# Column groups inside the K block, fewer zero matmuls, a modulation in two pieces and other wo banks, in an adaLN block of linear attention and GeGLU

## The chip, the cores and the metric

The kernel runs on one NeuronCore of a Trainium2 chip. The metric is the device time of one execution in microseconds. The engines are named as in the profile: PE is TensorE (PEld its weight loads), DVE is VectorE, ACT is ScalarE, POOL is GpSimd. The granted clock is the share of its full clock that TensorE was given, as the trace records it (1.0 is full, 0.5 is half; 128x512 matmuls start 0.216 us apart at 1.0 and 0.43 us apart at 0.5). A DMA lands when its data has arrived; to evict a PSUM bank is to read its result out of it, so that the bank can be written again.

## The reference, cut to what matters

```python
mod = (silu(c) @ w_mod).reshape(1, 6, 1, -1)        # sa, ca, ga, sb, cb, gb
h = layernorm(x) * (1 + ca) + sa                    # x: 2048 x 1024
x = x + ga * linear_attention(h, wqkv, wo)          # 32 heads, phi(t) = elu-like + 1e-6
h = layernorm(x) * (1 + cb) + sb
x = x + gb * (gelu(h @ w_gate) * (h @ w_up) @ w_down)   # F = 3584
```

The change touches the first half only: how sa and ca come about as columns, the K and V products of the first four chunks (128 rows each), the modulation of chunks 14 and 15, and the PSUM banks of the product with wo.

## The kernel before: the parts that matter

Work is recorded in program order, one in-order stream for each engine, and waits follow from the tiles that operations share. Where an operation stands in its engine's stream therefore matters as much as what it depends on: in the changed kernel one add of 0.16 us, standing early in DVE's stream, kept DVE idle for 2.25 us, and the work recorded behind it waited too.

```python
def mod_cols(q, bank):          # shift/scale of quarter q: 256 columns each, as 4 PSUM columns
    for t in range(2):
        for b in range(2):
            for dc in range(8):
                matmul(PS(bank, col, col + 1), WMQ[q][:, dc, t, b*128:(b+1)*128], SILUT[:, dc:dc+1], ...)
    DVE: MODT[:, q*4:q*4+4] = PS(bank, ...) + ADD4                              # L575

def warm(n, bank):              # n zero matmuls 128x512: they only keep PE active    L667
def mod1(c0, n, dc0, dc1):      # DVE: h1T = h1T * scale + shift, for each dc          L542
def k_part(q, cs):              # K matmuls of quarter q (dc = 2q, 2q+1) of chunks cs   L611
def xhat_dve(c), ln1_bn(c, h)   # DVE: normalise chunk c (L498); bn_stats of one half (L673)

# the head (cut)
t1(1, 6)                        # 8 PE transposes of chunk 1
warm(7, 7)
ln1_bn(2, 1); ln1_fin(2); ln1_bn(3, 0)
xhat_dve(2); t1(2, 7)
mod_cols(0, 4); mod1(0, 2, 0, 2)
...
warm(1); k_part(1, [0, 1, 2, 3])
warm(2)
mod_cols(2, 4); mod1(0, 4, 4, 6)
warm(1); k_part(2, [0, 1, 2, 3])
...
# the loop over chunks 4 to 15 (cut)
for _ in range({13: 1, 14: 1, 15: 0}.get(c_, 2)):
    q_block(...)                # takes the next of 4 PSUM banks; DVE evicts it (L601, L603)
# two K blocks, two V blocks, each in the next bank: with one q block, the second V reuses q's bank
if c_ % 2 == 1 and c_ + 2 < NCH:
    mod1(c_ + 1, 2)             # chunks c_+1 and c_+2 in one piece, 256 columns
if c_ == 13:
    ...                         # POOL builds the tile SEL: an iota and 4 tensor_scalar (L803)
if c_ >= 12:
    ...                         # DVE: two folds of wo with ga (L810)
# w2_pair(g): two matmuls into banks 2 and 3 (L840), ACT copies them to W2 (L842)
for c_ in range(12):
    wo_chunk(c_, 2 * ((c_ + 1) % 2))    # banks 2/3 first, then 0/1, ...             L928
```

Of the kernel before, what the change touches and what calls it, by code (L numbers as in the profile page):

```python
# [216 lines left out]
def bass_adaLN_cond__linear_attn_block__geglu_ffn__prompt_kernel(  # L217
# [14 lines left out]
    with ExitStack() as es:  # L232
# [264 lines left out]
        def xhat_dve(c_, dst, rng):  # L497
            sch.op(V, lambda e: e.tensor_scalar(dst[:, :], XALL[:, c_, :], MVA[:, c_, 0:1], RSA[:, c_:c_ + 1],  # L498
                                                op0=ALU.subtract, op1=ALU.mult),
                   rd=r_x(c_) + r_smc("mv", c_, 8) + r_smc("rs", c_, 4), wr=rng, note=f"xhat {c_}")  # L500
# [5 lines left out]
        def xh_buf(c_):  # L506
            i = c_ % 3
            return XH[i], r_2k(XHO[i], f"xh{i}")
# [10 lines left out]
        def t1(c_, tb):  # L519
            b_, rng = xh_buf(c_)  # L520
            sg, ci = divmod(c_, CPG)
            for dc in range(NDC):
                sch.op(T, lambda e, dc=dc: e.transpose(PS16(tb, dc * P, (dc + 1) * P), b_[:, dc * P:(dc + 1) * P], IDENT[:, :]),
                       rd=rng + r_sm("ident"), pwr=pr(tb), note=f"T1 {c_}.{dc}")
            sch.op(A, lambda e: e.activation(H1[sg][:, :, ci * P:(ci + 1) * P], PS16(tb).rearrange("p (a b) -> p a b", a=NDC), ACTF.Copy),
                   prd=pr(tb), wr=r_h1(sg, 0, NDC, ci * P, (ci + 1) * P), note=f"h1raw {c_}")
# [26 lines left out]
        def mod1(c0, n, dc0=0, dc1=NDC):  # L553
            sg, ci = divmod(c0, CPG)
            mods(H1, r_h1, sg, sc1, ci * P, (ci + n) * P, dc0, dc1, "h1")
# [109 lines left out]
        def warm(n, bank=None):  # L665
            for _ in range(n):
                sch.op(T, lambda e: e.matmul(PS(0 if bank is None else bank), WARM[:, 0:P], WARM[:, :], start=bank is not None,  # L667
                                             stop=bank is not None, skip_group_check=True),
                       rd=R_WARM, pwr=pr(bank) if bank is not None else (), note="warm")
# [5 lines left out]
        def ln1_fin(c_):  # L675
            sch.op(V, lambda e: e.bn_aggr(MVA[:, c_, :], STA[:, c_, :]), rd=r_smc("st", c_, 48), wr=r_smc("mv", c_, 8), note=f"aggr A{c_}")
            sch.op(V, lambda e: e.tensor_scalar(VEA[:, c_:c_ + 1], MVA[:, c_, 1:2], 1e-5, None, op0=ALU.add),
                   rd=r_smc("mv", c_, 8), wr=r_smc("ve", c_, 4), note=f"ve A{c_}")
            sch.op(G, lambda e: e.tensor_tensor(RSA[:, c_:c_ + 1], VEA[:, c_:c_ + 1], NEGHALF[:, :], ALU.pow),
                   rd=r_smc("ve", c_, 4) + r_sm("neghalf"), wr=r_smc("rs", c_, 4), deps=[last_g[0]], note=f"rstd A{c_}")  # L680
# [19 lines left out]
        ln1_bn(2, 0)  # L700
        xhat_dve(1, *xh_buf(1))
        t1(1, 6)
        warm(7, 7)
        ln1_bn(2, 1)
        ln1_fin(2)
        ln1_bn(3, 0)
        xhat_dve(2, *xh_buf(2))
        t1(2, 7)
        mod_cols(0, 4)
        mod1(0, 2, 0, 2)  # L710
        ln1_bn(3, 1)
        ln1_fin(3)
        k_part(0, [0, 1])
        xhat_dve(3, *xh_buf(3))
        mod1(2, 1, 0, 2)
        t1(3, 7)
        k_part(0, [2])
        mod1(3, 1, 0, 2)
        warm(3)
        k_part(0, [3])  # L720
        mod_cols(1, 4)
        mod1(0, 4, 2, 4)
        warm(1)
        k_part(1, [0, 1, 2, 3])
        warm(2)
        mod_cols(2, 4)
        mod1(0, 4, 4, 6)
        warm(1)
        k_part(2, [0, 1, 2, 3])
        warm(2)  # L730
        mod_cols(3, 4)
        mod1(0, 4, 6, 8)
        warm(1)
        k_part(3, [0, 1, 2, 3])
        for (c_, jg), b in kb0.items():
            k_evac(c_, jg, b)
# [26 lines left out]
        for c_ in range(4, NCH):  # L763
            if c_ % 4 == 0:
                q_todo += [(c_ // 4 - 1, qc) for qc in range(NG)]
            for _ in range({13: 1, 14: 1, 15: 0}.get(c_, 2)):
                q_block(*q_todo.pop(0))
            for jg in range(2):
                b = nb()
                kv_mm(c_, "k", jg, b, list(range(NDC)))  # L770
                k_evac(c_, jg, b)
            for jg in range(2):
                b = nb()
                kv_mm(c_, "v", jg, b, list(range(NDC)))
                v_evac(c_, jg, b)
            if c_ % 2 == 1 and c_ + 2 < NCH:
                mod1(c_ + 1, 2)
            kvacc(c_ - 1)
            if c_ + 3 < NCH:
                ln1(c_ + 3)  # L780
                t1d(c_ + 3)
            if c_ == 6:
                o_r = mod_rows(0, 4)
                for k, t in enumerate((6, 7, 8, 9)):
                    wm_dma(t, k)
                sch.dma(Q, lambda e: e.dma_start(GAB[:, :].rearrange("p (a b) -> p a b", a=2),
                                                 scr_row[0, 0:2, :].rearrange("(o a) b -> o a b", o=1).to_broadcast([P, 2, 512])),
                        wr=R_GAB, deps=[o_r], note="gab")
                sch.dma(Q, lambda e: e.dma_start(GBB[:, :].rearrange("p (a b) -> p a b", a=2),
                                                 scr_row[0, 2:4, :].rearrange("(o a) b -> o a b", o=1).to_broadcast([P, 2, 512])),  # L790
                        wr=R_GBB, deps=[o_r], note="gbb")
            if c_ == 9:
                o_r = mod_rows(1, 4)
                sch.dma(Q, lambda e: e.dma_start(SBT[:, :], scr_row[1, 0:2, :].rearrange("a (b p) -> p (a b)", p=P)),
                        wr=r_sm("sbT"), deps=[o_r], note="sbT")
                sch.dma(Q, lambda e: e.dma_start(CBT[:, :], scr_row[1, 2:4, :].rearrange("a (b p) -> p (a b)", p=P)),
                        wr=r_sm("cbT"), deps=[o_r], note="cbT")
                sch.dma(Q, lambda e: e.dma_start(WO[:], wo_v), wr=[(OFF_WS, OFF_WS + 16384, "wo")], note="wo")
            if c_ == 13:
                gop(lambda e: e.iota(IOTA_B[:].rearrange("p (a b d) -> p a b d", a=NG, b=HPG), [[4, NG], [1, HPG], [0, 32]],  # L800
                                     channel_multiplier=-1), wr=R_IOTA2)
                for k in range(4):
                    gop(lambda e, k=k: e.tensor_scalar(SEL[32 * k:32 * (k + 1)].rearrange("p a b -> p (a b)"), IOTA_B[32 * k:32 * (k + 1), :],  # L803
                                                       float(-32 * k), None, op0=ALU.is_equal), rd=R_IOTA2, wr=R_SEL)
            if c_ == 11:
                sch.op(V, lambda e: e.tensor_scalar(CB1T[:, :], CBT[:, :], 1.0, None, op0=ALU.add), rd=r_sm("cbT"), wr=r_sm("cb1T"))
            if c_ >= 12:
                for kc in range((c_ - 12) * 2, (c_ - 12) * 2 + 2):
                    rg = [(OFF_WS + kc * 2048, OFF_WS + (kc + 1) * 2048, "wo")]
                    sch.op(V, lambda e, kc=kc: e.tensor_tensor(WO[:, kc, :], WO[:, kc, :], GAB[:, :], ALU.mult),  # L810
                           rd=rg + R_GAB, wr=rg, note=f"wofold {kc}")
# [156 lines left out]
        for q in (4, 5, 6):  # L968
            wd_dma(q)
        for c_ in range(12):  # L970
            wo_chunk(c_, 2 * ((c_ + 1) % 2))
            if c_ == 0:
                den(1, 4)
            if c_ in (2, 3, 5, 6):
                bcast(1, (2, 3, 5, 6).index(c_))
            if c_ < 4:
                ln2_a(c_, False)
            if c_ == 9:
                mod2(0, 2)
                mod2(2, 2)  # L980
# [60 lines left out]
        for q in range(4):  # L1041
            hook(0, 5 + q, lambda q=q: wd_dma(q))
        for sg in range(NSG):
            gu_i[0] = 1 if sg == 0 else 0
            for fp in range(NFP):
                if fp + 2 < NFP and not (sg == 0 and fp == 0):
                    stream_pair(sg, fp + 2)
                ffn_fc(sg, 2 * fp)
                ffn_fc(sg, 2 * fp + 1)
                for fn in hooks.get((sg, fp), ()):  # L1050
                    fn()
            if sg + 1 < NSG:
                stream_pair(sg + 1, 0)
                stream_pair(sg + 1, 1)
            for ci in range(CPG):
                if sg + 1 < NSG:
                    n0 = (sg + 1) * CPG
                    if ci < 2:
                        ln2_a(n0 + 2 * ci, True)
                        ln2_a(n0 + 2 * ci + 1, True)  # L1060
                    else:
                        mod2(n0 + 2 * (ci - 2), 2)
                ffn_down(sg, ci)
# [74 lines left out]
```

## Time and profile before

| | before |
|---|---|
| time, median of 4 executions | 855.52 us (855.51 to 855.53) |
| PE busy | 837.3 of 853.6 us |
| first K matmul to first V matmul | 13.71 to 35.14 us |
| chunk 14's 16 K matmuls, to the first V matmul | 163.26 to 168.08 us |
| last w2 matmul to first wo matmul | 209.60 to 211.22 us |

From the profile's page: the busy time of the engines, and the chain of waits by engine.

```profile
PE 837.3 (98%) x4276; PEld 389.4 (46%) x4359; DVE 496.3 (58%) x881; ACT 294.8 (35%) x483; POOL 38.0 (4%) x73
...
PE 93%; DVE 4%; issue 1%; ACT 1%; POOL 0%; DMA 0%; SPq 0%; ACTq 0%; POOLq 0%
```

PE bounds the kernel. Where it runs freely, 128x512 matmuls start 0.216 us apart (their own 0.38 us overlap), so only places where this pitch is broken can be gained. Here is the head, in the timeline of PE (start, length, engine, line, operation, out<-in, shapes, count, and in brackets the idle time before it and its releaser):

```profile
9.59 1.67 PE L667 MATMUL ps_all<-warm 128*128 128x512 bf16 x7
11.37 0.62 PE L523 MATMUL ps_all<-ident,xh 128*128 128x128 bf16 x8
11.83 0.94 PE L569 MATMUL ps_all<-siluT,wmq 128*128 128x1 bf16 x32
13.71 1.67 PE L611 MATMUL ps_all<-wk,h1T 128*128 128x512 bf16 x7 [0.94 <-DVE h1T L542]
...
23.62 0.94 PE L569 MATMUL ps_all<-siluT,wmq 128*128 128x1 bf16 x32
24.43 0.38 PE L667 MATMUL ps_all<-warm 128*128 128x512 bf16 x1
25.50 2.97 PE L611 MATMUL ps_all<-wk,h1T 128*128 128x512 bf16 x13 [0.69 <-DVE h1T L542]
...
35.14 1.03 PE L611 MATMUL ps_all<-wv,h1T 128*128 128x512 bf16 x4
```

In every quarter PE computes the columns and then waits for DVE to put them onto h1T. In quarters 1 to 3 a zero matmul stands in between, although matmuls of the quarter before could have filled that time. The second place is around chunk 13 and 14, in the timeline of all engines:

```profile
154.09 11.68 POOL L803 TENSOR_SCALAR sel<-iota_b 32x1024 bf16<-32x1024 int32 x4
154.21 3.18 DVE L810 TENSOR_TENSOR wo<-wo,gab 128x1024 bf16<-128x1024 bf16 x2
...
157.31 1.25 DVE L601 TENSOR_SCALAR eb<-eb 128x512 f32<-128x512 f32 x1
...
158.60 0.69 DVE L603 SCALAR_TENSOR_TENSOR pq<-ps_all,eb 128x512 bf16<-128x512 f32 x1
...
162.10 3.82 DVE L542 TENSOR_SCALAR h1T<-h1T,modt 128x256 bf16<-128x256 bf16 x8
...
164.17 1.16 PE L611 MATMUL ps_all<-wk,h1T 128*128 128x512 bf16 x4 [0.31 <-DVE h1T L542]
...
165.91 2.33 PE L611 MATMUL ps_all<-wk,h1T 128*128 128x512 bf16 x10 [0.59 <-DVE h1T L542]
...
168.08 3.62 PE L611 MATMUL ps_all<-wv,h1T 128*128 128x512 bf16 x16
```

DVE reaches the modulation of chunk 14 only at 162.10, and the 16 K matmuls take 4.82 us instead of 16 x 0.216 = 3.45: 1.37 us are lost. L601 took 1.25 us while POOL built SEL (a mask for a later product); at 168.11, without POOL beside it, it took 0.41. The third place is the start of wo, in the timeline of PE:

```profile
209.39 0.59 PE L840 MATMUL ps_all<-wo,kvt 128*128 128x512 bf16 x2
211.22 2.12 PE L928 MATMUL ps_all<-w,pq 128*128 128x512 bf16 x8 [1.23 <-ACT w L842]
```

The first wo chunk uses banks 2 and 3, which ACT is still emptying: 1.62 us from start to start instead of 0.22.

### The profile page before, as it was taken

What the parts mean: (1) busy time and instruction counts of PE and PEld (TensorE: products, weight loads), DVE (VectorE), ACT (ScalarE), POOL (GpSimd) and SP (SyncE); (2) the same over time, 40 slices, a digit from 0 to 9 for tenths busy, and PEclk for the clock granted to TensorE, in tenths of its full rate; (3) what the DMA queues carried; (4) which work ended last, traced back from release to release, by engine and by line L of the source; (5) the groups of instructions that cost most, each with busy time, mean ns of one, the idle gap of its engine ahead of it and who ended that gap; (6) DMA issues with size and microseconds to landing.
All of it is one profiled execution on the core that took longest, in us unless ns stands there. A gap on an engine that the chain in (4) does not pass through costs nothing.

```text
span 853.6 us, 11465 instructions
## 1 busy us (share of the span) xinstructions
PE 837.3 (98%) x4276; PEld 389.4 (46%) x4359; DVE 496.3 (58%) x881; ACT 294.8 (35%) x483; POOL 38.0 (4%) x73
## 2 busy tenths in 40 slices
PE   7999999999999999999999999999999999999998
PEld 3454444443444444444444444444444444444445
DVE  5577667978674455564365666445666535655512
ACT  2233333335513344430245443035454204454300
POOL 2010000600200000000000001000000100000000
PEclk9999999999999999999999999999999999999999
DMA  9981924003523368341355534145553305555000
GB/s 281 362 257 26 272 32 117 13 1 96 178 74 99 99 199 254 109 117 44 112 153 149 149 99 100 36 120 158 157 159 106 72 25 154 149 149 147 6 20 25
DMA packets 179911, 104.06 MB, mean 122 GB/s; under 512 B 32520, under 2 KB 171912, under 8 KB 179856
## 3 DMA queue, kind: packets, MB, share of 16 engines
q1 hardware_dynamic: 179856, 103.33, 43.5%
q8 instruction: 35, 0.57, 0.3%
q14 instruction: 20, 0.16, 0.1%
HBM read 92.28 MB, written 4.21 MB: 113 GB/s over the span
## 4 chain that ended last, share of the span: by engine, by line
PE 93%; DVE 4%; issue 1%; ACT 1%; POOL 0%; DMA 0%; SPq 0%; ACTq 0%; POOLq 0%
PE ps_all L997 23%; PE ps_all L1022 23%; PE ps_all L994 21%; PE ps_all L611 11%; PE ps_all L928 6%; PE ps_all L652 6%; DVE h1T L542 1%; PE ps_all L633 1%; DVE eb L601 0%; PE ps_all L868 0%; PE ps_all L583 0%; DVE xh L498 0%; DVE st L673 0%; DMA xall<-in_A_x_dram 0%; DVE pq L881 0%
## 5 line engine op out<-in xcount | busy, mean ns | idle before, releaser
L997 PE MATMUL ps_all<-h2T,wu 128*128 128x512 bf16 x896 | 339.6, 379 | 1.7
L994 PE MATMUL ps_all<-h2T,wg 128*128 128x512 bf16 x863 | 327.1, 379 | 0.0
L1022 PE MATMUL ps_all<-wd,yT 128*128 128x512 bf16 (+1 forms) x906 | 193.2, 372 | 0.9
L1005 ACT ACTIVATE q<-ps_all 128x512 f32<-128x512 f32 x112 | 66.9, 597 | 235.2 <-PE ps_all L994 231.3
L1022 PEld LDWEIGHTS ps_all<-wd,yT 128*128 128x128 bf16 x924 | 90.4, 98 | 103.3
L994 PEld LDWEIGHTS ps_all<-h2T,wg 128*128 128x128 bf16 x896 | 87.7, 98 | 105.8 <-issue 0.2
L997 PEld LDWEIGHTS ps_all<-h2T,wu 128*128 128x128 bf16 x896 | 87.7, 98 | 105.7
L1007 DVE SCALAR_TENSOR_TENSOR ww<-q,ps_all 128x512 f32<-128x512 f32 x112 | 77.0, 688 | 92.5 <-ACT guh L1006 92.5
L1010 DVE SCALAR_TENSOR_TENSOR ww<-th,guh 128x512 f32<-128x512 f32 x112 | 77.5, 692 | 77.9 <-ACT th L1009 77.9
L1009 ACT ACTIVATE th<-ww 128x512 f32<-128x512 f32 x112 | 70.5, 629 | 84.4 <-DVE ww L1007 84.4
L1012 DVE TENSOR_TENSOR yT<-ww,ps_all 128x512 bf16<-128x512 f32 x112 | 76.8, 686 | 3.8
L1027 DVE TENSOR_TENSOR ps_all<-ps_all,gbb 128x512 f32<-128x512 f32 (+1 forms) x33 | 22.5, 682 | 94.8 <-PE ps_all L1022 94.8
L600 ACT ACTIVATE eb<-ps_all 128x512 f32<-128x512 f32 x64 | 37.5, 601 | 85.0 <-PE ps_all L611 43.6
L1006 ACT ACTIVATE guh<-ps_all 128x512 f32<-128x512 f32 x112 | 66.2, 591 | 0.0
L611 PE MATMUL ps_all<-wk,h1T 128*128 128x512 bf16 x250 | 58.1, 379 | 3.9 <-DVE h1T L542 3.7
L928 PE MATMUL ps_all<-w,pq 128*128 128x512 bf16 x246 | 56.2, 379 | 1.9 <-ACT w L842 1.2
L611 PE MATMUL ps_all<-wv,h1T 128*128 128x512 bf16 x254 | 57.6, 379 | 0.1
L652 PE MATMUL ps_all<-h1T,wq 128*128 128x512 bf16 x243 | 56.6, 379 | 1.0 <-issue 0.3
L601 DVE TENSOR_SCALAR eb<-eb 128x512 f32<-128x512 f32 x64 | 28.8, 449 | 29.7 <-ACT eb L600 29.2
L611 PEld LDWEIGHTS ps_all<-wk,h1T 128*128 128x128 bf16 x256 | 24.6, 98 | 33.6 <-DVE h1T L542 5.7
L928 PEld LDWEIGHTS ps_all<-w,pq 128*128 128x128 bf16 x256 | 24.6, 98 | 31.6 <-ACT w L842 1.7
L611 PEld LDWEIGHTS ps_all<-wv,h1T 128*128 128x128 bf16 x256 | 24.9, 98 | 29.9 <-DVE pq L603 0.3
(87 smaller groups left out, 423.3 us busy)
## 6 DMA issues: line engine op xcount, KB each, us to landing
wg<-in_B_w_gate_dram SPq DMA_DIRECT2D x56, 512.0 KB, 3.9
wu<-in_B_w_up_dram SPq DMA_DIRECT2D x56, 512.0 KB, 5.2
wmst<-in_w_mod_dram SPq DMA_DIRECT2D x8, 1024.0 KB, 11.7
wd<-in_B_w_down_dram SPq DMA_DIRECT2D x7, 1024.0 KB, 7.8
wmq<-in_w_mod_dram SPq DMA_DIRECT2D x8, 512.0 KB, 6.7
out_dram<-xall SPq DMA_DIRECT2D x31, 128.0 KB, 1.7
xall<-in_A_x_dram SPq DMA_DIRECT2D x3, 1024.0 KB, 12.3
wk<-in_A_wqkv_dram SPq DMA_DIRECT2D x4, 512.0 KB, 8.2
```

What stands on the lines that cost most here:

```text
L611: o = sch.op(T, lambda e, dc=dc: e.matmul(PS(bank), H1[sg][:, dc, ci * P:(ci + 1) * P], W_[:, dc, jg * 512:(jg + 1) * 512], start=(dc == 0 ...
L652: o = sch.op(T, lambda e, dc=dc: e.matmul(PS(b), WQ[:, dc, qc * P:(qc + 1) * P], H1[sg][:, dc, :], start=(dc == 0), stop=(dc == NDC - 1)), ...
L928: last[half] = sch.op(T, lambda e, g=g, half=half: e.matmul(PS(b0 + half), PQ[sg][:, g, ci * P:(ci + 1) * P], W2[:, g, half * 512:(half + ...
L994: og = sch.op(T, lambda e, dc=dc: e.matmul(PS(bg), WG[slot][:, dc, e_ * P:(e_ + 1) * P], H2[sg][:, dc, :], start=(dc == 0), stop=(dc == ND ...
L997: ou = sch.op(T, lambda e, dc=dc: e.matmul(PS(bu), WU[slot][:, dc, e_ * P:(e_ + 1) * P], H2[sg][:, dc, :], start=(dc == 0), stop=(dc == ND ...
L1005: sch.op(A, lambda e: e.activation(Q1[j][:, :], PS(bg), ACTF.Square, scale=math.sqrt(GELU_A)), prd=pr(bg), wr=rq, note=f"q1 {fc}")
L1006: ogh = sch.op(A, lambda e: e.activation(GUH[j][:, :], PS(bg), ACTF.Copy, scale=0.5), prd=pr(bg), wr=rg, note=f"gh {fc}")
L1007: sch.op(V, lambda e: e.scalar_tensor_tensor(WW[j][:, :], Q1[j][:, :], 1.0, PS(bg), op0=ALU.add, op1=ALU.mult), rd=rq, prd=pr(bg), wr=rw, ...
L1009: sch.op(A, lambda e: e.activation(TH[j][:, :], WW[j][:, :], ACTF.Tanh, scale=GELU_C), rd=rw, wr=rt, note=f"th {fc}")
L1010: sch.op(V, lambda e: e.scalar_tensor_tensor(WW[j][:, :], TH[j][:, :], 1.0, GUH[j][:, :], op0=ALU.add, op1=ALU.mult), rd=rt + rg, wr=rw, n ...
L1012: sch.op(V, lambda e: e.tensor_tensor(YT[:, fc, :], WW[j][:, :], PS(bu), ALU.mult), rd=rw, prd=pr(bu), wr=r_yt(fc), note=f"yT {fc}")
L1022: o = sch.op(T, lambda e, b=b, fc=fc, c0=c0, c1=c1, n=n: e.matmul(PS(b, 0, n), YT[:, fc, ci * P:(ci + 1) * P], WDT[fc // 4][:, fc % 4, c0:c1],
```

## The change

Its intent: compute the columns of the next quarter in the middle of the K matmuls of the present one, so that the trip over DVE is covered by useful matmuls, and drop the zero matmuls that filled it; bring chunk 14's modulation forward, as a piece of its own; begin wo in free banks. The diff, cut to its core, with the cut marked:

```diff
         t1(1, 6)
-        warm(7, 7)
+        warm(1, 7)
+        mod_cols(0, 4)
         ln1_bn(2, 1)
         ln1_fin(2)
         ln1_bn(3, 0)
         xhat_dve(2, *xh_buf(2))
+        mod1(0, 2, 0, 2)
         t1(2, 7)
-        mod_cols(0, 4)
-        mod1(0, 2, 0, 2)
 ...                                  # [cut: chunks 2 and 3 of quarter 0, same idea, warm(3) dropped]
         warm(1)
-        k_part(1, [0, 1, 2, 3])
-        warm(2)
+        k_part(0, [3])
+        k_part(1, [0, 1, 2])
         mod_cols(2, 4)
         mod1(0, 4, 4, 6)
+        k_part(1, [3])
         warm(1)
-        k_part(2, [0, 1, 2, 3])
-        warm(2)
+        k_part(2, [0, 1])
         mod_cols(3, 4)
         mod1(0, 4, 6, 8)
-        warm(1)
+        k_part(2, [2, 3])
         k_part(3, [0, 1, 2, 3])
@@ loop over chunks
+            if c_ == 13:
+                mod1(14, 1)
             for _ in range({13: 1, 14: 1, 15: 0}.get(c_, 2)):
                 q_block(*q_todo.pop(0))
@@
-                mod1(c_ + 1, 2)
+                mod1(*((15, 1) if c_ == 13 else (c_ + 1, 2)))
@@ wo
-            wo_chunk(c_, 2 * ((c_ + 1) % 2))
+            wo_chunk(c_, 6 if c_ == 0 else 2 * (c_ % 2))
@@ first gate/up pair of banks
-            gu_i[0] = 1 if sg == 0 else 0
+            gu_i[0] = 0
```

## The prediction

> **What bounds it.** TensorE. The page gives PE 837.3 of 853.6 us busy (98%), clock 1.0, and the chain of waits is 93% PE. In the timeline dense 128x512 matmuls start 0.216 us apart, so only places where the pitch is broken can give time. I see three that the change touches.
> 1. Head (first K block): matmuls start at 13.71 us, V starts at 35.14 us: 21.4 us. Inside are 64 K matmuls (13.8 us), 8 transposes (0.45), three column groups (0.9 each), so 4.4 us are zero matmuls (10 x 0.216) and waits for the scale/shift (list of waits: 3.7 us in 6 waits, partly elsewhere).
> 2. Chunk 14: its K matmuls wait for the DVE modulation (L542); 16 take 4.82 us (163.26 to 168.08) instead of 3.45: 1.37 us lost.
> 3. First wo chunk: starts at 211.22, 1.62 us after the last w2 matmul, waiting for ACT to empty banks 2/3 (L842): 1.40 us lost.
>
> **Costed.**
> Head. The first column group moves before T1(2) and its add (L575) stands before bn_stats of chunk 2 on DVE. Weight columns wmq0 land only at 10.7 us (DMA issues: 6.4 and 7.6 us to landing), so DVE waits from 9.1 to about 11.3, xhat(2) moves from 10.77 to about 13.3, and K begins about 0.6 us LATER (14.3). After that each group runs as soon as its PE slot comes, ahead of the quarter's last matmuls, and 8 of 10 zero matmuls go. Stepping through with trace durations (group to column 1.2 us, column to first matmul 0.67 us): quarter 1 at 19.6, quarter 2 at 24.1, quarter 3 at 28.0 (was 30.38), V at 32.8. Landings permit it (wmq2 20.9, wmq3 25.1, x4-7 36.2 us; wv estimated 29.9 and 33.1). Gain 2.3 us, all critical.
> wo. Chunk 0 in banks 6/7 starts at once; W2[7] is ready (211.2) before its last two matmuls. Gain 1.4 us. Re-dealing the others is symmetrical.
> Chunk 14. Splitting makes 8 extra DVE operations (128 columns, 0.22 us pitch each, hardly cheaper than 256 columns at 0.26). mod(14) now stands before chunk 13's q eviction. There DVE is already behind (xhat 15, two wo folds until 157.3), and GpSimd builds SEL 154.1 to 165.8: L601 takes up to 1.25 us instead of 0.42. [...] The second V block of chunk 13 uses q's bank and already starts just as that eviction ends (159.34). Estimate: mod(14) takes 2.8 us there, so that block stalls about 2.8 us, while K 14 no longer stalls: net LOSS 1.4 us (from 1.4 gained, if DVE has slack I don't see, to 2.3 lost).
>
> **Sum.** 855.5 - 2.3 - 1.4 + 1.4 = 853.2; with some chance of a clock drop and of a smaller loss at chunk 13: **853.2 us, range 850.4 to 855.3**. Chances: faster by over 2% 0.01, within 2% 0.98, slower 0.01.
>
> **What would show it.** Timeline: K begins near 14.3, V near 32.8. PE after the last w2 matmul: pitch 0.22, no wait on L842. Waits: PE on DVE L603 of 2 to 3 us in chunk 13's V; no L542 wait in chunk 14. FFN windows unchanged.
>
> **What would make it wrong.** (a) Clock. [...] From 9.8 to 14.3 us PE now does only 32 one-column matmuls and 8 transposes; before, this stretch was 11.3 to 13.7 and the clock held. A drop would cost 1 to 3 us (0.43 us pitch, as at the start). I give it 15%. (b) mod(14) runs quickly: then near 851. (c) DVE order in the head costs more than I stepped through.

855.5 - 2.3 - 1.4 + 1.4 = 853.2; no term was for the clock, only the range.

## The result, and the profile after

The changed kernel took 855.87 us in the median of 4 executions (856.29, 856.15, 854.55, 855.59); the kernel before, in the same rounds, 855.52. The ratio is 1.0001, with a 95% interval of 0.9984 to 1.0019: no change. (A ratio is the mean time of one kernel's fast runs over that of the other's of the same rounds, so not quite the ratio of the medians.) The range, 850.4 to 855.3, was missed. One thing stands out before any trace is read: in these rounds the kernel before repeats within 0.02 us at a granted clock of 1.0, the changed one spreads over 1.7 us, and its executions show clocks of 0.994, 0.994, 0.996 and 0.996.

The head, in the timeline of all engines:

```profile
9.87 0.54 PE L569 MATMUL ps_all<-siluT,wmq 128*128 128x1 bf16 x16
10.79 0.55 PE L569 MATMUL ps_all<-siluT,wmq 128*128 128x1 bf16 x16 [0.38 <-DMA wmq<-in_w_mod_dram]
11.38 0.16 DVE L575 TENSOR_TENSOR modt<-ps_all,add 128x4 f32<-128x4 f32 x1 [2.25 <-PE ps_all L569]
...
13.24 0.55 DVE L498 TENSOR_SCALAR xh<-xall,mv,rs 128x1024 bf16<-128x1024 bf16 x1
...
13.84 1.03 PE L523 MATMUL ps_all<-ident,xh 128*128 128x128 bf16 x8 [2.50 <-DVE xh L498]
...
14.67 5.07 PE L611 MATMUL ps_all<-wk,h1T 128*128 128x512 bf16 x12
...
28.98 6.20 PE L611 MATMUL ps_all<-wk,h1T 128*128 128x512 bf16 x28
...
35.02 7.07 PE L611 MATMUL ps_all<-wv,h1T 128*128 128x512 bf16 x32
```

DVE stood 2.25 us before the first add, PE then stood 2.50 us before T1(2), both much as predicted. But the first twelve K matmuls take 5.07 us, a pitch of 0.43 us instead of 0.216. The busy times by stretch show the reason; the columns are the stretch and its length, busy us (and count) of PE, PEld, DVE, ACT and POOL, the granted clock, the share of DMA and GB/s:

```profile
9.10:12.51 3.41, 1.77 (x41) 1.48 (x41) 1.10 (x6) 1.02 (x1) 0.00 (x0) 1.00 1.12 325
12.51:15.93 3.42, 2.09 (x11) 1.29 (x12) 2.69 (x8) 1.02 (x1) 1.07 (x2) 0.50 1.14 324
15.93:19.34 3.41, 3.41 (x9) 1.21 (x8) 0.99 (x3) 0.00 (x1) 0.03 (x1) 0.50 1.21 303
...
159.29:162.70 3.41, 1.43 (x8) 0.64 (x8) 3.34 (x9) 0.60 (x1) 3.33 (x2) 1.00 0.00 0
162.70:166.11 3.41, 3.41 (x16) 1.76 (x15) 3.38 (x9) 0.60 (x1) 3.33 (x2) 0.50 0.03 7
```

The clock halves twice, for 6.83 us in the head and for 3.41 us near chunk 13, each time after a stretch in which PE was busy for about half of it or less. The second time it follows a stall that the change itself made:

```profile
153.98 12.13 POOL L803 TENSOR_SCALAR sel<-iota_b 32x1024 bf16<-32x1024 int32 x4
...
157.19 3.04 DVE L542 TENSOR_SCALAR h1T<-h1T,modt 128x128 bf16<-128x128 bf16 x8
...
160.16 0.42 DVE L601 TENSOR_SCALAR eb<-eb 128x512 f32<-128x512 f32 x1
160.61 0.69 DVE L603 SCALAR_TENSOR_TENSOR pq<-ps_all,eb 128x512 bf16<-128x512 f32 x1
...
161.35 2.32 PE L611 MATMUL ps_all<-wv,h1T 128*128 128x512 bf16 x8 [1.98 <-DVE pq L603]
...
164.33 2.78 PE L652 MATMUL ps_all<-h1T,wq 128*128 128x512 bf16 x8
...
166.94 3.62 PE L611 MATMUL ps_all<-wk,h1T 128*128 128x512 bf16 x16
```

mod(14), 3.04 us long beside POOL, stands in front of chunk 13's q eviction, and the second V block waits for that eviction's bank. Chunk 14's K then runs without a wait, as intended. The start of wo is as intended too (timeline of PE):

```profile
211.70 0.59 PE L840 MATMUL ps_all<-wo,kvt 128*128 128x512 bf16 x2
212.13 2.11 PE L928 MATMUL ps_all<-w,pq 128*128 128x512 bf16 x9
```

The ledger of the two profiled executions, by the start of a matmul of each stage:

| from | to | before | after | difference |
|---|---|---|---|---|
| start | first V | 35.14 | 35.02 | -0.12 |
| first V | key-value accumulation of chunk 13 (L633) | 136.39 | 138.83 | +2.44 |
| that | last w2 matmul | 38.07 | 38.06 | -0.01 |
| last w2 | first wo | 1.62 | 0.22 | -1.40 |
| first wo | first gate matmul | 45.15 | 45.14 | -0.01 |

Summed, the first gate matmul comes 0.90 us later (257.27 against 256.37), and the span is 0.9 us longer (854.5 against 853.6).

### The profile page after: what moved, and what is told of

Its sections match the earlier page's. It is cut to its first block, busy times and chain, and to the rows that moved or that the text cites. A ratio compares the mean times of both kernels' runs of the same rounds, so it can differ in the third digit from the quotient of the medians.

```text
span 854.5 us, 11526 instructions
## 1 busy us (share of the span) xinstructions
PE 842.5 (99%) x4345; PEld 389.9 (46%) x4345; DVE 496.9 (58%) x889; ACT 294.8 (35%) x483; POOL 38.4 (4%) x73
## 4 chain that ended last, share of the span: by engine, by line
PE 96%; DVE 2%; DMA 1%; issue 0%; SPq 0%; ACT 0%; POOL 0%; ACTq 0%; POOLq 0%
PE ps_all L1022 23%; PE ps_all L994 23%; PE ps_all L997 23%; PE ps_all L611 13%; PE ps_all L928 7%; PE ps_all L652 6%; DMA wmq<-in_w_mod_dram 1%; PE ps_all L633 1%; PE ps_all L868 0%; PE ps_all L583 0%; DVE h1T L542 0%; PE ps_all L840 0%; PE ps_all L523 0%; DVE pq L881 0%; PE ps_all L569 0%
## 5 line engine op out<-in xcount | busy, mean ns | idle before, releaser
L994 PE MATMUL ps_all<-h2T,wg 128*128 128x512 bf16 x896 | 339.6, 379 | 0.0
L611 PE MATMUL ps_all<-wk,h1T 128*128 128x512 bf16 x256 | 60.5, 390 | 0.5 <-DVE h1T L542 0.5
L652 PE MATMUL ps_all<-h1T,wq 128*128 128x512 bf16 x256 | 59.8, 383 | 0.0
L601 DVE TENSOR_SCALAR eb<-eb 128x512 f32<-128x512 f32 x64 | 27.9, 436 | 31.9 <-ACT eb L600 31.5
```

What stands on the lines that cost most here:

```text
L611: o = sch.op(T, lambda e, dc=dc: e.matmul(PS(bank), H1[sg][:, dc, ci * P:(ci + 1) * P], W_[:, dc, jg * 512:(jg + 1) * 512], start=(dc == 0 ...
L652: o = sch.op(T, lambda e, dc=dc: e.matmul(PS(b), WQ[:, dc, qc * P:(qc + 1) * P], H1[sg][:, dc, :], start=(dc == 0), stop=(dc == NDC - 1)), ...
L994: og = sch.op(T, lambda e, dc=dc: e.matmul(PS(bg), WG[slot][:, dc, e_ * P:(e_ + 1) * P], H2[sg][:, dc, :], start=(dc == 0), stop=(dc == ND ...
```

## The experiments

Two questions were open. In the head: does the rearranged K block gain what was predicted when the clock holds, or do the trips over DVE and the DMA landings eat the gain, with the clock a side show? At chunk 13: is the stall due to eight more DVE operations in a bad place, or to POOL, beside which DVE is slow there (L601 1.25 us, 0.41 without it)? All ratios are against the kernel before in the same rounds, five rounds each. "V" is the start of the first V matmul in the profiled execution; the last column lists the granted clock of the five executions, each 0.002 below 1 being about 3.41 us at half clock (0.5 x 3.41 of 854 us; the profiled execution of e11 shows one such stretch and 0.998, that of the changed kernel three and 0.994). (The profiled execution of e4 holds no clock record and is listed as 1.0; the pitch of its matmuls agrees, with eight K matmuls in 1.89 us.)

| run | median us (range) | ratio (95% interval) | V | clocks |
|---|---|---|---|---|
| e1 zero matmuls back | 852.44 (851.94 to 854.72) | 0.9970 (0.9958 to 0.9983) | 32.34 | 1.0 x3, 0.998 x2 |
| e2 split undone | 853.71 (853.34 to 854.84) | 0.9981 (0.9968 to 0.9995) | 34.88 | 0.996 x3, 0.997, 0.998 |
| e3 both | 851.71 (851.14 to 852.21) | 0.9956 (0.9944 to 0.9969) | 32.81 | 1.0 x5 |
| e4 zero matmuls, SEL early | 849.86 (849.18 to 851.73) | 0.9938 (0.9925 to 0.9950) | 32.41 | 1.0 x4, 0.998 |
| e5 before + SEL early | 854.10 (854.08 to 854.14) | 0.9984 (0.9971 to 0.9996) | 35.22 | 1.0 x4, 0.999 |
| e6 before + wo banks | 854.13 (854.00 to 854.57) | 0.9985 (0.9972 to 0.9999) | 35.17 | 1.0 x5 |
| e7 four zero matmuls | 854.38 (852.46 to 855.49) | 0.9986 (0.9973 to 0.9998) | 33.09 | 1.0, 0.998 x2, 0.996 x2 |
| e8 SEL early, no split | 850.65 (850.03 to 852.50) | 0.9945 (0.9933 to 0.9958) | 33.19 | 1.0 x4, 0.998 |
| e9 add after xhat | 849.86 (848.80 to 851.38) | 0.9935 (0.9922 to 0.9947) | 31.84 | 1.0 x3, 0.998 x2 |
| e10 filled, no split | 849.89 (849.24 to 850.33) | 0.9932 (0.9918 to 0.9945) | 32.29 | 1.0 x4, 0.998 |
| e11 before + split | 857.94 (856.17 to 857.97) | 1.0024 (1.0011 to 1.0036) | 35.21 | 1.0, 0.998 x3, 0.997 |

### e1: ten zero matmuls put back into the gap

```diff
         warm(1, 7)
         mod_cols(0, 4)
+        warm(10, 7)
```

> Changed kernel plus ten zero matmuls right after the first column group, in the 2.5 us in which TensorE now sits idle. Clock theory: the head's clock stays 1.0 in every execution, K starts near 14.3 us and V near 32.8 to 33.0 us instead of 35.0; the time falls by about 2 us against the changed kernel, to about 853.9 if chunk 13 still stalls and drops its clock, less where it does not. Rival (the hand-over over VectorE and the DMA landings set the head, the clock only looks like it): V stays at 34.5 to 35.2 us with the clock at 1.0, and the time does not move by more than 0.3 us.

Measured: 852.44 us. The timeline of PE:

```profile
10.80 2.32 PE L667 MATMUL ps_all<-warm 128*128 128x512 bf16 x10
...
13.89 2.75 PE L611 MATMUL ps_all<-wk,h1T 128*128 128x512 bf16 x12
...
32.34 1.03 PE L611 MATMUL ps_all<-wv,h1T 128*128 128x512 bf16 x4
```

Work that computes nothing makes the kernel 3.4 us faster than the changed one (852.44 against 855.87). The twelve K matmuls now take 2.75 instead of 5.07 us, and V starts 2.68 us earlier. The rival is out: with the clock held, the head gains what was predicted. In this execution chunk 13 stalled for the same 1.98 us and the clock did not drop; two other executions show 0.998, which no profile places. This experiment came out faster than expected because the median execution had no second drop.

### e2: the split undone

```diff
-            if c_ == 13:
-                mod1(14, 1)
...
-                mod1(*((15, 1) if c_ == 13 else (c_ + 1, 2)))
+                mod1(c_ + 1, 2)
```

> Changed kernel with the modulation of chunks 14 and 15 put back into one piece at its old place; head and wo banks as in the changed kernel. Clock theory: no stall of 2.0 us in chunk 13's V, no clock drop near 162 us, the wait of 1.4 us in chunk 14's K is back; head still drops (V near 35.0). About 854.0 us, and little spread. Rival (the split is worth its intended 1.4 us and the loss lies elsewhere): 855.9 + 1.4 = 857.3 us.

Measured: 853.71 us. From first V to the accumulation of chunk 13 it takes 136.39 us, as before the change, and the clock does not drop there; the head's drop stays (V at 34.88; the profiled execution has a clock of 0.996, as two half-clock stretches of 3.41 us give) and all five clocks are below 1. The split is a loss, and the loss of 2.4 us is found.

### e3: both

```diff
         mod_cols(0, 4)
+        warm(10, 7)
...
-            if c_ == 13:
-                mod1(14, 1)
...
+                mod1(c_ + 1, 2)             # in place of the split, as in e2
```

> Both of the above together: clock 1.0 throughout, V near 32.9 us, 1.4 us wait in chunk 14, wo chunk 0 without wait. Clock theory: 855.5 - 2.2 - 1.4 = 851.9 us, with a spread under 0.1 us. If the head's gain never existed: 854.1 us.

Measured: 851.71 us, clock 1.0 in all five executions. V is at 32.81 (predicted 32.8). The spread, 1.1 us, is not the 0.1 expected: its likely source is the landing of the first column weights, on which the first add, and with it K, now hangs. In this profiled execution PE waits for them until 11.26 us; in that of e1 it does not wait for them at all (the 32 one-column matmuls run through from 10.00 us), and K starts 0.88 us and V 0.47 us earlier. Two profiles of two kernels do not prove it for the other executions.

### e4: zero matmuls, and POOL's work moved to chunk 9

```diff
         mod_cols(0, 4)
+        warm(10, 7)
...
-            if c_ == 13:
+            if c_ == 9:
                 gop(lambda e: e.iota(IOTA_B[:] ...      # and the four tensor_scalar of SEL
```

> Changed kernel with the ten zero matmuls and with GpSimd's building of SEL (12 us) moved from chunk 13 to the end of chunk 9, where VectorE has slack; the split modulation stays. [...] wo folds, xhat and modulation run at 1.2, 0.55 and 0.22 us again, chunk 13's V and chunk 14's K both run without a wait, no clock drop near 162 us; 851.9 - 1.4 = 850.5 us. Rival (eight more VectorE operations in front of the eviction are the cause whatever GpSimd does): a stall of 1.8 us or more stays in chunk 13's V, time at or above 852.5 us.

Under test is whether DVE is late at chunk 13 because POOL builds SEL beside it.

Measured: 849.86 us, 0.6 us below what was expected (850.5). The timeline of DVE at the same place in the program:

```profile
150.71 2.35 DVE L811 TENSOR_TENSOR wo<-wo,gab 128x1024 bf16<-128x1024 bf16 x2
152.98 1.87 DVE L542 TENSOR_SCALAR h1T<-h1T,modt 128x128 bf16<-128x128 bf16 x8
...
155.21 0.69 DVE L603 SCALAR_TENSOR_TENSOR pq<-ps_all,eb 128x512 bf16<-128x512 f32 x1
```

The folds take 2.35 instead of 3.18 us and mod(14) 1.87 instead of 3.04, the q eviction comes in time, and neither chunk 13's V nor chunk 14's K waits: 135.00 us from V to the accumulation of chunk 13, 3.83 us less than in the changed kernel. The place of the eight operations is harmless when DVE is not behind.

### e5: only POOL's work moved, in the kernel before

```diff
-            if c_ == 13:
+            if c_ == 9:
                 gop(lambda e: e.iota(IOTA_B[:] ...
```

> The kernel before with one edit: GpSimd's building of SEL moved from chunk 13 to the end of chunk 9. [...] VectorE is about 3 us earlier at chunk 14, its undivided modulation is done before chunk 14's K asks for it, the 1.4 us wait there vanishes without any split: 854.1 us. Rival (the split[...] is what removes that wait): the wait stays at 1 us or more and the time at 855.3 to 855.6 us.

Measured: 854.10 us; also 135.00 us from V to chunk 13's accumulation. The timeline of PE shows no wait in chunk 13's V or in chunk 14's K:

```profile
157.68 3.62 PE L611 MATMUL ps_all<-wv,h1T 128*128 128x512 bf16 x16
...
163.31 2.97 PE L611 MATMUL ps_all<-wk,h1T 128*128 128x512 bf16 x13
```

The wait that the split was meant to remove vanishes without the split. Its cause was POOL's work at that place. How POOL slows DVE is not shown; what is measured in the kernel before is that beside SEL the pair of wo folds took 3.18 us (2.34 after it) and L601 up to 1.25 (0.41 after it), while L603 took 0.69 both times.

### e6: only the wo banks, in the kernel before

```diff
-            wo_chunk(c_, 2 * ((c_ + 1) % 2))
+            wo_chunk(c_, 6 if c_ == 0 else 2 * (c_ % 2))
...
-            gu_i[0] = 1 if sg == 0 else 0
+            gu_i[0] = 0
```

> The kernel before with the wo banks (and the matching first gate/up pair) of the changed one and nothing else: 1.40 us less, 854.1 us; first wo matmul 0.22 us after the last w2 matmul, the L842 wait gone, no clock drop. If the wait only moved to the eighth row group (which needs the last w2 copy), the gain is under 0.7 us.

Measured: 854.13 us, 0.22 us from the last w2 matmul to the first wo matmul, no clock drop: the full 1.40 us in this stage, and 1.3 us in the median (855.44 before).

### e7: four zero matmuls instead of ten

```diff
         mod_cols(0, 4)
+        warm(4, 7)
```

> Changed kernel plus four zero matmuls (0.9 us of work) after the first column group instead of ten, leaving TensorE idle for 1.6 us before T1(2). A check of how sparse a stretch may be: if a mostly busy window is enough, the head drop disappears in most executions (granted clock 0.998 or 1.0, 852.0 to 854.0 us, V near 32.5); if any idle stretch of this kind trips the clock, it stays in all (V near 35, clock 0.994 to 0.996, 854.5 to 856.3 us). I expect a mixture, depending on where the window falls.

The window meant is the 3.41 us between steps of the clock in the changed kernel's trace (12.51, 19.34, 162.70 and 166.11 us, 2, 42 and 1 times 3.413 us apart).

Measured: 854.38 us with clocks of all three kinds. The profiled execution kept its clock in the head, in spite of 1.61 us without work before T1(2), and lost it at chunk 13 (busy times by stretch, columns as above):

```profile
12.70:16.11 3.41, 1.80 (x15) 0.95 (x14) 3.18 (x10) 0.86 (x1) 0.55 (x1) 1.00 1.16 313
156.06:159.47 3.41, 1.43 (x8) 0.47 (x7) 3.38 (x11) 0.94 (x2) 3.33 (x2) 1.00 0.00 0
159.47:162.89 3.42, 3.42 (x9) 1.22 (x10) 3.35 (x8) 0.00 (x0) 3.34 (x2) 0.50 0.03 7
```

Two executions show 0.996, so more than one window ran at half clock in them; where, only a profile of them could tell. Four are not dependable.

### e8: SEL early, and no split

The edits of e3 and e4 together:

```diff
         mod_cols(0, 4)
+        warm(10, 7)
...
-                mod1(14, 1)                 # and mod1(c_ + 1, 2) again, as in e2
...
-            if c_ == 13:
+            if c_ == 9:                     # SEL, as in e4
```

> Changed kernel with ten zero matmuls in the head, SEL early, and the modulation of chunks 14 and 15 undivided at its old place. [...] with VectorE in time the split is worth nothing; no wait in chunk 13's V or chunk 14's K, 849.9 us, equal to the run with the split within 0.3 us. Rival (split needed as well): a wait of about 1 us in chunk 14's K, 850.9 us.

Measured: 850.65 us. From V to chunk 13's accumulation it takes 135.00 us, the very number of e4: the split is worth nothing once POOL is out of the way. The time missed the expected 0.3 us around 849.9. In the profiled execution the first column weights landed at 11.6 us against 10.8 in e4, and V came 0.78 us later; the rest is the same.

### e9: the first add behind xhat, no added zero matmuls

```diff
-        mod_cols(0, 4)                  # matmuls, then DVE's add
+        add0 = mod_cols(0, 4, True)     # matmuls; the add is recorded later
         ln1_bn(2, 1)
         ln1_fin(2)
         ln1_bn(3, 0)
         xhat_dve(2, *xh_buf(2))
+        add0()
         mod1(0, 2, 0, 2)
```

SEL is early as in e4, the split stays.

> Changed kernel, no zero matmuls added, SEL early, and VectorE's add of the first columns placed after bn_stats and xhat of chunk 2 rather than before them. If the idle 2.5 us in the head come from that order alone, T1(2) starts at 11.4 us instead of 13.8, K at about 12.3 us, the head drop is gone without zero matmuls, and V starts near 31.6 us, limited by landings of wmq1, wmq2, wmq3; total about 849.1 us. If order is not the cause, V stays above 32.4 us or the clock drops again (851 us or more).

Measured: 849.86 us, 0.8 us over what was expected (849.1), though the head is better than with ten zero matmuls. The timeline of PE:

```profile
11.63 0.61 PE L523 MATMUL ps_all<-ident,xh 128*128 128x128 bf16 x8
12.72 2.75 PE L615 MATMUL ps_all<-wk,h1T 128*128 128x512 bf16 x12 [0.49 <-DVE h1T L542]
...
31.84 4.51 PE L615 MATMUL ps_all<-wv,h1T 128*128 128x512 bf16 x19
```

T1(2) follows the first column group at once, so the idle 2.5 us were made by the place of one 0.16 us add in DVE's stream. The profiled execution took 849.53 us; two of five executions still show a clock of 0.998.

### e10: as e9, undivided modulation, six zero matmuls where PE waits

```diff
-        warm(1, 7)
+        warm(3, 7)                  # before the first column group
...
         t1(2, 7)
+        warm(2, 0)
...
-        warm(1)                     # after the second column group
+        warm(3)
```

> Columns' first add after xhat of chunk 2, SEL early, modulation undivided, wo banks re-dealt, and six zero matmuls laid only where TensorE waits anyway (two before the first column group, two after T1(2), two after the second group). V near 31.8 us as without them, no clock drop in any execution if mostly filled windows are enough: 849.3 us with a spread under 1 us. If zero matmuls in the head cost their 0.22 us each: 850.6 us.

Measured: 849.89 us, 0.6 us over what was expected (849.3), with a spread of 1.1 us and one execution at 0.998. The zero matmuls cost nothing visible: the first K matmul is at 12.77 us, in e9 at 12.72. V at 32.29 is later than in e9 because the column weights landed later: PE waits 0.54 us for them at 21.66, in e9 0.16 us at 21.23. It is the narrowest of e4, e9 and e10, which do not differ in the median: all three are 0.6 to 0.7% faster than the kernel before in the same rounds, and by as much than the changed one, which ran in other rounds.

### e11: only the split, in the kernel before

```diff
+            if c_ == 13:
+                mod1(14, 1)
             for _ in range({13: 1, 14: 1, 15: 0}.get(c_, 2)):
...
-                mod1(c_ + 1, 2)
+                mod1(*((15, 1) if c_ == 13 else (c_ + 1, 2)))
```

> The kernel before with the split modulation of chunks 14 and 15 and nothing else. My stepping through: a stall of 2.0 us in chunk 13's V, the 1.4 us wait of chunk 14's K gone: plus 0.6 us, 856.1 us, in executions without a clock drop; up to 857.9 us where the clock drops for one window near 162 us. If the split were right as intended: 854.1 us.

Measured: 857.94 us. The execution at clock 1.0 took 856.17 us, the four others 857.91 to 857.97. The profiled one shows the 1.99 us stall in chunk 13's V, no wait in chunk 14's K, and half clock from 162.04 to 165.45 us. So the split by itself costs 0.6 us (855.61 before; one execution), and 2.3 us with the clock drop that its stall brings on.

## Why the prediction was wrong, point by point

- **What bounds the kernel, and the three places:** right. The rest of the ledger moved by 0.01 us.
- **wo, -1.4 us:** right, in the changed kernel (-1.40) and alone (e6: -1.40 in this stage, 854.13 against 855.44 us in the median).
- **Head, -2.3 us:** the stepping through was right and the gain did not come. K began at 14.67 us (predicted 14.3) because DVE waited for the landing of the first column weights, as predicted. With the clock held, V starts at 32.34, 32.81 and 33.09 us (e1, e3, e7), around the predicted 32.8. In the changed kernel it starts at 35.02, because 6.83 us of the head ran at half clock. The step that failed is the prediction's point (a), "A drop would cost 1 to 3 us ... I give it 15%". The size was right: 2.2 us against the head of e3. The chance was not: all four executions of the changed kernel and all five of e2, which has the same head, show a clock below 1. The prediction had the sparse stretch, 9.8 to 14.3 us, in hand, and reasoned that it would likely pass because a shorter one had.
- **Chunk 13, +1.4 us:** the mechanism was right, with two sizes off. The stall was 1.98 us instead of 2.8, and the net loss 0.6 instead of 1.4: mod(14) took 3.04 us, but L601 behind it then took 0.42 instead of 1.25, so part of POOL's delay was only moved, not added. Net that is +0.6 us at full clock (e11, 856.17 us), or +0.77 in the stage as e1's profile has it (137.16 us from V to chunk 13's accumulation, the stall without a drop). The drop that follows in most executions was not foreseen at all: the prediction looked for clock drops in the head alone. With it the stage cost 2.44 us in the profiled execution, and the alternative in which the split gains 1.4 us never came near.
- **Sum:** the parts without clock drops are -2.3, +0.6 to +0.8 and -1.4 us, near 852.5; e1, which differs from the changed kernel by the ten zero matmuls, took 851.94 to 852.44 us in its three executions at clock 1.0, inside the forecast range. The two clock drops made the difference: in the profiled execution 2.2 us in the head (against e3) and 1.67 us at chunk 13 (138.83 against e1's 137.16), which brings 852.5 to 856.4, against 856.29 measured. The median, 855.87, also holds two executions with a clock of 0.996, about two half-clock windows instead of three; where they lay, no profile shows.

**What the traces say of the clock, and what stays open.** The steps of the clock in the changed kernel's trace, at 5.69, 12.51, 19.34, 162.70 and 166.11 us, are 2, 2, 42 and 1 times 3.413 us apart, and the half clock of e7 (159.47 to 162.89) and e11 (162.04 to 165.45) lasted 3.41 us, so PE's busy time can be added up window by window on this raster. After the start-up, where the clock is first raised (at 7.48 us in the kernel before, 5.69 in the changed one), these windows at full clock were followed by half clock: with 1.43 or 1.44 us of PE work (changed kernel at 159.29, e7 at 156.06, e11 at 158.62) and 1.77 us (changed kernel at 9.10). All other windows at full clock of the kernels before and changed, up to 845 us, were followed by full clock; the sparsest of them had 2.16 us (before, at 208.86). In the experiments windows with 1.80 us (e7 at 12.70) and 1.82 us (e1 at 154.87) held it. In these traces the line therefore lies near 1.8 us, about half of a window; this is an estimate from the windows named. Where the half-clock window was then full (3.41 us of work near chunk 13), the clock was back after one; in the head, where it had 2.09 us, only after two. The line would also say why the same 1.98 us stall cost e1 nothing: by the reading of e1's raster (a border at 158.28 us) it lay across the border of two windows, from 156.69 to 158.67 us, and in the changed kernel, e7 and e11 wholly inside one. e11, at 856.17 us once and 857.9 four times, fits this, though its fast execution was not profiled. That the line is so sharp is not shown: PE's busy time is modelled, and 1.09 of the 1.77 us are one-column matmuls, of which no run shows how they count. That they count for nothing does not fit: e7's window from 9.29 us held its clock with 2.26 us, of which 1.10 were one-column matmuls, and the other 1.16 alone would be less than the 1.43 us that dropped. Nor is it known where the executions of e4, e8, e9 and e10 with a clock of 0.998 lost it, as none of these was profiled.

## What to carry to other kernels

Before you remove zero matmuls or move work, add up PE's busy time over every stretch of 3.4 us, wherever it may begin, and not only the single gaps: here half clock followed windows with 1.43 to 1.77 us and not those with 1.80 us or more, and a stall of 2 us cost up to 1.8 us more by way of the clock (e11: 857.94 us in the median, 856.17 in the execution at clock 1.0). A spread of times where there was none, with granted clocks of 0.994 to 0.998, pointed to this before any trace was read. And where an engine is late, ask first what slows it: moving POOL's 12 us of work away removed a wait for nothing that a rearrangement of DVE's stream only shifted to another place, and made worse.
